# Two more blocks by seven products at two levels, and sums on GpSimd, in an attention and feed-forward kernel

## The chip, the cores and the metric

One core of a Trainium2 chip runs the whole kernel. The metric is device time in microseconds of one execution. All data are float32.

## What is computed

```python
def reference(q, k, v, g_norm, w_in, w_out, s, b):      # q, k, v: (8, 8, 576, 64)
    kv = np.einsum('bhsd,bhse->bhde', k, v)
    out = np.einsum('bhsd,bhde->bhse', q, kv)
    rms = np.sqrt(np.mean(out * out, axis=-1, keepdims=True) + 1e-06)
    x = (out / rms * g_norm).transpose(0, 2, 1, 3).reshape(4608, 512)
    h = x @ w_in                                        # (4608, 512) @ (512, 2048)
    r = np.maximum(h, 0.0)
    return (s * (r * r) + b) @ w_out                    # (4608, 2048) @ (2048, 512)
```

The attention has no softmax: per batch and head a 64x64 matrix kv, and its product with q, normalized row by row. Then comes a feed-forward layer of width 2048 whose activation is an affine function of the squared ReLU.

## The kernel before

**Units.** The 4608 tokens are done in nine units of 512. The code counts them u = 0 to 8; the text calls them units 1 to 9. A unit has a first half (x to the hidden activations, `mm1`) and a second half (hidden to output, `mm2`). Beside them, with steps placed by hand, runs the attention of the next unit (`attention_of_two`, L517, for two pairs of 128 tokens called A and B): turn, product, back, square, row sum, norm, turn_x, scale. The kv product of a batch (`kv_product`, L366) is done where it is due.

**Seven products.** Each matrix product is done by a scheme with seven products of half-size blocks in place of eight. With A the weights and B the activations, cut into 2 x 2 blocks, the products are numbered 1: A11 B11, 2: A12 B21, 3: S4 B22, 4: A22 T4, 5: S1 T1, 6: S2 T2, 7: S3 T3. S1 to S4 are sums of blocks of A, T1 to T4 of B (T1 = B12 - B11, T2 = B22 - T1, T3 = B22 - B12, T4 = B21 - T2). In PSUM one accumulator takes products 1, 6, 5, 3 in that order and is read off after each; a second takes 7 and 4, and product 2 has its own.

**First half of units 3 to 9** (`mm1_deep`, L815 to L1055). The hidden width is cut into four slices s = 0 to 3, which make two pairs, 0 (slices 0, 1) and 1 (slices 2, 3). `x1`, `x6`, `x5` (L849 to L868) do products 1, 6, 5 of one slice, each with four matmul instructions of 256 columns. `small(i, pair, *ms)` (L889) does product i (2, 3, 4 or 7) of both slices of a pair at once, by the scheme a second time: its seven small products m are two matmul instructions of 128 columns each. Before the change, products 2 and 3 are done so for both pairs and 4 and 7 for pair 0; `y7` and `y4` (L859, L877) do 7 and 4 for slices 2 and 3 one slice at a time, four instructions of 256 columns each. The list of those done twice is `DEEP` (L314); their weight sums (two parts each, `sums_of_w_in`, L786) are computed in unit 2, stored to DRAM, and read back in each later unit.

The activations T4 and T3 of a unit are `xs_4` and `xs_7`, computed at the end of the unit before (`x_sums`, L609). `sums_of_x` and `sums_of_xs(i)` (L820, L837) compute the second level's sums of them, four operations each, into tiles `sub`. The hidden blocks are `a11`, `a21`, `a12`, `a22`; `a12` and `a22` (L870, L873) add the parts, `s1` and `s3` (L882, L886) make the sums that the second half needs. Two operations for each slice (square and affine, `done`, L963) are ScalarE's.

**Banks.** `small` for products 2 and 3 writes its first accumulator to one bank (`sx_ps`, a single buffer) and the second to another (`z_ps`, single); a new m = 1 must wait until m = 3 of the call before has been read, and a new m = 2 or 7 until the `z` use before has been read. For product 4 the accumulators are in two buffers `st_ps`, for 7 in two buffers `y_ps`.

**Order.** Nothing is scheduled: each engine executes its instructions in the order in which the code issues them, and waits for what an instruction needs. `run` (L968) is that order for the first half; `at(n)` are the attention's steps, listed in `sides` (L1765 on). The second half starts with `rest` (L1431), into which the last calls of `small` are threaded (`p3_5`, `p3_34`). It ends with four groups of four output stores (`store`, L1269).

**Queues.** SP's queue reads weights through a ring of 14 slots (`pump`, L1088, in the order of `queue_w2`, L1081; a slot is given back in that order by `used`, L1117). GpSimd's queue issues the reads of q (`loads`, L1689; 16 or 32 transfers for one call), the output stores, in unit 2 the stores of weight sums of the second half (`parts_of_w`, L1155), and two memsets a unit (`start_5`, L1395).

Of the kernel before, what the change touches and what calls it, by code (L numbers as in the profile page):

```python
# [17 lines left out]
def kernel(  # L18
# [240 lines left out]
    def add(o, a, b):  # L259
        nc.vector.tensor_tensor(out=o, in0=a, in1=b, op=ALU.add)  # L260

    def sub(o, a, b):
        nc.vector.tensor_tensor(out=o, in0=a, in1=b, op=ALU.subtract)  # L263
# [50 lines left out]
    DEEP = ((2, 0), (7, 0), (3, 0), (4, 0), (2, 1), (3, 1))  # L314
# [321 lines left out]
    ga, g_pair = {}, {}  # L636
# [27 lines left out]
    def g_tile(name, s):  # L664
        if s % 2 == 0:
            g_pair[name, s // 2] = gp.tile([P, 2, 2, TB], FP32, name=name, tag=name)
        ga[name, s] = g_pair[name, s // 2][:, s % 2]
        return ga[name, s]
# [146 lines left out]
    def mm1_deep(u):  # L815
# [4 lines left out]
        def sums_of_x():  # L820
# [8 lines left out]
            sub(t1, b12, b11)  # L829
            sub(t2, b22, t1)  # L830
            sub(t3, b22, b12)
            sub(t4, b21, t2)
# [4 lines left out]
        def sums_of_xs(i):  # L837
# [4 lines left out]
            sub(t1, b12, b11)  # L842
            sub(t2, b22, t1)
            sub(t3, b22, b12)
            sub(t4, b21, t2)
# [13 lines left out]
        def y7(s):  # L859
            st["y", s] = bank_of("y", "y")  # L860
            mm1_product(7, u, s, st["y", s], True)

        def seventh(s):
            return ga["a22", s] if s < 2 else st["y", s]
# [5 lines left out]
        def a12(s):  # L870
            add(g_tile("a12", s), seventh(s), st["r2", s])

        def a22(s):  # L873
            t = ga["a22", s] if s < 2 else g_tile("a22", s)
            add_relu(t, seventh(s), ga["a21", s])

        def y4(s):  # L877
            mm1_product(4, u, s, st["y", s], False)
            t = g_tile("a12", s)
            add_relu(t, st["y", s], st["r2", s])  # L880

        def s1(s):  # L882
            g_tile("s1", s)
            g_s1(s)

        def s3(s):  # L886
            sub(ga["a21", s], ga["a11", s], ga["a21", s])

        def small(i, pair, *ms):  # L889
            name = {2: "a11", 3: "a21", 4: "a12", 7: "a22"}[i]  # L890
            g = (i, pair)
            apart = g == (4, 0)
            fresh = i == 7
            if fresh and ms[0] == 1:
                for s in (2 * pair, 2 * pair + 1):
                    g_tile(name, s)
# [4 lines left out]
            def w_of(m):  # L901
                s0, s1 = 2 * pair, 2 * pair + 1
                raw = {1: (s0, 0), 2: (s0, 1), 4: (s1, 1)}
                if m in raw:
                    s, k = raw[m]
                    return w_in_deep(i, s)[:, k]
                n, k = {6: (6, 0), 7: (6, 1), 5: (5, 0), 3: (5, 1)}[m]
                return ring[u, g, n][:, k]

            def bank_for(m):  # L910
                if fresh:
                    ps = bank_of(("s", i, m), "y").rearrange("p b (m c) -> p (b m) c", c=P)
                    return ps[:, :2]
# [9 lines left out]
            def keep(n, j, h):  # L923
                tag = f"q{n}t" if apart or fresh else {1: "r14", 2: "r2_2", 4: "q4"}[n]
                st[g, n] = late["tmp"].tile([P, 2, P], FP32, name="r", tag=tag)
                if fresh:
                    nc.scalar.copy(st[g, n], st[g, "x"])  # L927
                else:
                    add(st[g, n], st[g, "x"], to(j, h))

            def last(j, h, ps, r):
                (add if fresh else add_relu)(to(j, h), ps, r)

            for m in ms:
# [4 lines left out]
                w, x = w_of(m), a[i, m]  # L939
# [8 lines left out]
                elif m == 2:  # L948
                    last(0, 0, ps, st[g, 1])
                elif m == 6:  # L950
                    keep(2, 1, 0)
                elif m == 5:
                    keep(4, 1, 1)
                    last(1, 1, st[g, "y"], st[g, 4])
                elif m == 3:
                    if fresh:
# [953 lines left out]
```

## Time and profile before

| | us |
|---|---|
| median of 3 runs (898.35 to 899.75) | 898.79 |
| the profiled execution | 898.25 |
| its span in the profile | 896.5 |
| TensorE busy | 886.0 |
| VectorE, ScalarE, GpSimd busy | 697.4, 353.6, 262.2 |
| start of `x1(0)` of units 3 to 9 in the span | 236.4, 329.2, 424.3, 519.6, 614.7, 710.0, 802.6 |

The page gives each engine's busy time, its share in 40 slices of the span, the chain that ended last, and groups of like instructions with count, busy time, mean duration and the idle time before them with what ended it. The timeline gives start, duration, engine, line and operation, with the idle time in front and its releaser in brackets; a run of like instructions is one row. PE is TensorE, DVE is VectorE, ACT is ScalarE, POOL is GpSimd, and SP is the engine that only issues transfers. The time is about 1.8 us longer than the span.

### The profile page before, as it was taken

The numbers are of one execution on the slowest core, as the hardware profiler recorded it, in microseconds if no ns is written. First come the engines' busy times: TensorE is split into PE (matmuls) and PEld (weight loads), VectorE is DVE, ScalarE is ACT, GpSimd is POOL, SyncE is SP. The second block draws the span as 40 slices with busy tenths as digits, with TensorE's granted clock in tenths as the row PEclk, the third lists the DMA queues.
The fourth block names the chain that finished last, engine by engine and source line by source line (L and its number), as shares of the span: only waits on it lengthen the run. The fifth ranks groups of instructions, "written<-read, shape, count | busy, mean of one in ns | idle before, by whom it ended". The sixth has DMA issues, their size and how long they took to land.

```text
span 896.5 us, 19936 instructions
## 1 busy us (share of the span) xinstructions
PE 886.0 (99%) x7706; PEld 819.3 (91%) x7706; DVE 697.4 (78%) x1374; ACT 353.6 (39%) x612; POOL 262.2 (29%) x493
## 2 busy tenths in 40 slices
PE   7999999999999999999999999999999999999998
PEld 4888888888899999999899999999999999999998
DVE  2898777885697978798778868887879797975696
ACT  2887023522266005630455026601660066105610
POOL 2028057014662024701481027403520300021000
PEclk9999999999999999999999999999999999999999
DMA  9897739449963986389646974597639822993286
GB/s 263 310 336 234 197 93 289 162 129 346 305 191 102 311 299 190 87 267 329 215 100 207 310 253 110 153 318 244 186 106 305 294 75 60 301 312 93 60 283 188
DMA packets 124109, 192.96 MB, mean 215 GB/s; under 512 B 25712, under 2 KB 43504, under 8 KB 124016
## 3 DMA queue, kind: packets, MB, share of 16 engines
q1 hardware_dynamic: 104048, 165.84, 57.9%
q0 software_dynamic: 16512, 23.63, 9.3%
q10 hardware_dynamic: 3456, 2.23, 1.0%
q8 instruction: 61, 1.00, 0.5%
q14 instruction: 32, 0.26, 0.1%
HBM read 164.37 MB, written 27.26 MB: 214 GB/s over the span
## 4 chain that ended last, share of the span: by engine, by line
PE 95%; DVE 3%; DMA 1%; ACT 0%; issue 0%; SPq 0%; DVEq 0%
PE x_ps L92 47%; PE y_ps L92 25%; PE z_ps L92 11%; PE sx_ps L92 6%; PE st_ps L92 2%; PE y_ps L553 2%; PE kv_ps L385 2%; DMA kv_sb<-in_v_dram 1%; DVE xT L597 0%; DVE xn L586 0%; DVE xs L263 0%; DVE xn L474 0%; SPq L107 0%; PE z_ps L385 0%; DVE ss L464 0%
## 5 line engine op out<-in xcount | busy, mean ns | idle before, releaser
L1693 POOL DMA_DIRECT2D q_sb<-in_q_dram x296 | 167.1, 572 | 83.1 <-ACT r L927 43.2
L1273 POOL DMA_DIRECT2D out_dram<-o x120 | 59.4, 502 | 358.7 <-issue 210.5
L92 PE MATMUL x_ps<-w_sb,sub 128*128 128x128 f32 x1176 | 148.5, 275 | 0.0
L92 PEld LDWEIGHTS x_ps<-w_sb,sub 128*128 128x128 f32 x1176 | 139.8, 192 | 0.0
L652 ACT ACTIVATE a<-a,b_col,s_col 128x512 f32<-128x512 f32 x144 | 117.1, 814 | 26.9 <-DVE a L655 18.6
L852 ACT COPY a<-x_ps 128x512 f32<-128x512 f32 x28 | 16.3, 581 | 243.1 <-PE x_ps L92 243.1
L92 PE MATMUL x_ps<-xs,ws_raw 128*128 128x256 f32 x384 | 91.4, 381 | 0.1
L92 PE MATMUL x_ps<-xT,wa 128*128 128x256 f32 x360 | 84.1, 382 | 0.1
L92 PE MATMUL y_ps<-xs,wb 128*128 128x256 f32 (+1 forms) x360 | 80.0, 365 | 0.0
L92 PEld LDWEIGHTS x_ps<-xs,ws_raw 128*128 128x128 f32 x384 | 69.5, 190 | 8.5 <-ACT r L726 0.5
L92 PEld LDWEIGHTS x_ps<-xT,wa 128*128 128x128 f32 x360 | 66.6, 190 | 10.7 <-issue 1.7
L965 ACT ACTIVATE a<-a 128x512 f32<-128x512 f32 x112 | 69.5, 621 | 5.5 <-DVE a L267 5.5
L92 PEld LDWEIGHTS y_ps<-xs,wb 128*128 128x128 f32 x360 | 62.9, 190 | 9.1 <-issue 2.3
L92 PE MATMUL x_ps<-w_sb,a 128*128 128x128 f32 (+1 forms) x432 | 64.9, 298 | 0.0
L92 PE MATMUL y_ps<-w_sb,a 128*128 128x128 f32 (+1 forms) x416 | 62.4, 295 | 0.0
L92 PEld LDWEIGHTS x_ps<-w_sb,a 128*128 128x128 f32 x432 | 58.4, 192 | 2.9 <-issue 0.4
L92 PEld LDWEIGHTS y_ps<-w_sb,a 128*128 128x128 f32 x416 | 56.0, 192 | 2.1
L260 DVE TENSOR_TENSOR r<-sx_ps,a 128x256 f32<-128x256 f32 x84 | 35.2, 419 | 23.4 <-PE sx_ps L92 23.3
L260 DVE TENSOR_TENSOR r<-x_ps,o 128x256 f32<-128x256 f32 (+1 forms) x84 | 29.6, 353 | 28.5 <-PE x_ps L92 27.8
L92 PE MATMUL y_ps<-w_sb,sub 128*128 128x128 f32 x392 | 49.5, 275 | 0.0
L92 PE MATMUL z_ps<-w_sb,a 128*128 128x128 f32 (+1 forms) x352 | 46.9, 280 | 0.0
L263 DVE TENSOR_TENSOR a<-a,a 128x512 f32<-128x512 f32 x72 | 46.7, 683 | 0.1
(232 smaller groups left out, 1645.9 us busy)
## 6 DMA issues: line engine op xcount, KB each, us to landing
w_sb<-w SPq DMA_DIRECT2D x427, 256.0 KB, 4.9
w_sb<-w SPq DMA_DIRECT2D x14, 512.0 KB, 8.0
w<-sub POOLq DMA_DIRECT2D x28, 256.0 KB, 5.0
out_dram<-o POOLq DMA_DIRECT2D x112, 64.0 KB, 4.2
w_sb<-in_k_dram SPq DMA_DIRECT2D x24, 288.0 KB, 4.6
w_sb<-in_v_dram SPq DMA_DIRECT2D x24, 288.0 KB, 4.7
w_raw<-in_moe_w_in_dram SPq DMA_DIRECT2D x6, 1024.0 KB, 9.0
q_sb<-in_q_dram POOLq DMA_DIRECT2D x160, 32.0 KB, 3.8
```

The costliest lines, as they stand in the source:

```text
L92: nc.tensor.matmul(o, lhsT=lhsT, rhs=rhs, start=start, stop=stop, skip_group_check=True)
L260: nc.vector.tensor_tensor(out=o, in0=a, in1=b, op=ALU.add)
L263: nc.vector.tensor_tensor(out=o, in0=a, in1=b, op=ALU.subtract)
L385: nc.tensor.matmul(ps[r][(r ^ l) * HB : (r ^ l) * HB + HB, i, :], lhsT=kv[l][0][rows, j, :], rhs=kv[l][1][rows, j, :], start=(j == 0), sto ...
L553: nc.tensor.matmul(ps[l][32 * p : 32 * p + 32, r, lo:hi], lhsT=bd_kv[b % 2][rows, p, at : at + 32], rhs=st["qT"][rows, p, lo:hi], start=Tr ...
L652: nc.scalar.activation(t, t, AF.Identity, scale=s_col, bias=b_col)
L852: nc.scalar.copy(g_tile("a11", s), st["x", s])
L965: nc.scalar.square(ga[name, s], ga[name, s])
L1273: queues[s % 2].dma_start(out=view[b, jj, :, cols], in_=st[name, j][s * w : s * w + w, cols])
L1693: load()
```

## The change

In units 3 to 9, products 7 (S3 T3) of both pairs are done by the scheme twice and in lockstep (`seven`, with a full bank for both pairs), and product 4 (A22 T4) of pair 1 also by `small`; `y7` and `y4` go. `DEEP` grows by (7, 1) and (4, 1), whose sums unit 2 computes in its second half. The twelve sums of x, and s1 and s3 of slices 0 and 1, are GpSimd's. The order in `run` is new; the last two small products of (4, 1) move into `rest` (`p4_34`); the reads of q that were at step 15 are at 18; the kv product of unit 4 is later (`kv3`). Kept parts of product 4 and 7 share buffers, and one of the second half's moves to the buffer `rb`.

```diff
@@ -311,7 +311,7 @@
 
     w2_dram = [dram.tile([P, 2, FC // 2, P], FP32, name=f"w2_{i}") for i in range(8)]
     w3_dram = [dram.tile([P, 4, FC // 4, P], FP32, name=f"w3_{i}") for i in range(8)]
-    DEEP = ((2, 0), (7, 0), (3, 0), (4, 0), (2, 1), (3, 1))
+    DEEP = ((7, 0), (7, 1), (2, 0), (3, 0), (4, 0), (2, 1), (4, 1), (3, 1))
...
@@ -662,7 +662,11 @@
         affine(t)
 
     def g_tile(name, s):
-        if s % 2 == 0:
+        if name == "a22":
+            if s == 0:
+                g_all[0] = gp.tile([P, 2, 2, 2, TB], FP32, name=name, tag=name, bufs=1)
+            g_pair[name, s // 2] = g_all[0][:, s // 2]
+        elif s % 2 == 0:
             g_pair[name, s // 2] = gp.tile([P, 2, 2, TB], FP32, name=name, tag=name)
         ga[name, s] = g_pair[name, s // 2][:, s % 2]
         return ga[name, s]
@@ -826,10 +830,10 @@
                 late["sub"].tile([P, FC // 4, P], FP32, name="sub", tag="sub", bufs=6) for _ in range(2)
             ]
             (t1, t2), (t3, t4) = ((x[:, :2], x[:, 2:]) for x in t)
-            sub(t1, b12, b11)
-            sub(t2, b22, t1)
-            sub(t3, b22, b12)
-            sub(t4, b21, t2)
+            sub(t1, b12, b11, nc.gpsimd)
+            sub(t2, b22, t1, nc.gpsimd)
+            sub(t3, b22, b12, nc.gpsimd)
+            sub(t4, b21, t2, nc.gpsimd)
...
@@ -856,61 +860,79 @@
             st["r2", s] = rp.tile([P, 2, TB], FP32, name="r2", tag="ra" if s % 2 else "rb")
             nc.scalar.copy(st["r2", s], st["x", s])
-        def y7(s):
-            st["y", s] = bank_of("y", "y")
-            mm1_product(7, u, s, st["y", s], True)
-
-        def seventh(s):
-            return ga["a22", s] if s < 2 else st["y", s]
+        def seven(*ms):
+
+            if ms[0] == 1:
+                for t in range(NS):
+                    g_tile("a22", t)
+
+            def to(j, h):
+                return g_all[0][:, :, j, :, h * P : h * P + P]
+
+            def keep(n):
+                st[7, n] = late["tmp"].tile([P, 2, 2, P], FP32, name="r", tag="q2t" if n == 2 else "q14t")
+                nc.scalar.copy(st[7, n], st[7, "x"])
+
+            for m in ms:
+                first = m in (1, 2, 7)
+                if first:
+                    ps = bank_of(("s", 7, m), "y").rearrange("p b (m c) -> p (b m) c", c=P)
+                    st[7, "x" if m == 1 else "y"] = ps.rearrange("p (i b) c -> p i b c", b=2)
+                ps = st[7, "x" if m in (1, 6, 5, 3) else "y"]
+                for pair in range(2):
+                    w = w_deep(7, pair, m)
+                    for b in range(2):
+                        matmul(ps[:, pair, b], w[:, b], a[7, m], first and pair + b == 0, True)
+                    if m in (7, 3):
+                        used((u, (7, pair), 6 if m == 7 else 5))
+                if m == 1:
+                    keep(1)
+                elif m == 2:
+                    add(to(0, 0), ps, st[7, 1])
+                elif m == 6:
+                    keep(2)
+                elif m == 5:
+                    keep(4)
+                    add(to(1, 1), st[7, "y"], st[7, 4])
+                elif m == 3:
+                    nc.scalar.copy(to(0, 1), ps)
+                elif m == 4:
+                    add(to(1, 0), ps, st[7, 2])
 
         def x5(s):
             mm1_product(5, u, s, st["x", s], False)
             nc.scalar.copy(g_tile("a21", s), st["x", s])
 
         def a12(s):
-            add(g_tile("a12", s), seventh(s), st["r2", s])
+            add(g_tile("a12", s), ga["a22", s], st["r2", s])
 
         def a22(s):
-            t = ga["a22", s] if s < 2 else g_tile("a22", s)
-            add_relu(t, seventh(s), ga["a21", s])
-
-        def y4(s):
-            mm1_product(4, u, s, st["y", s], False)
-            t = g_tile("a12", s)
-            add_relu(t, st["y", s], st["r2", s])
-
-        def s1(s):
-            g_tile("s1", s)
-            g_s1(s)
-
-        def s3(s):
-            sub(ga["a21", s], ga["a11", s], ga["a21", s])
+            add_relu(ga["a22", s], ga["a22", s], ga["a21", s])
+
+        def s1(s, engine=nc.vector):
+            add(g_tile("s1", s), ga["a21", s], ga["a22", s], engine)
+
+        def s3(s, engine=nc.vector):
+            sub(ga["a21", s], ga["a11", s], ga["a21", s], engine)
+
+        def w_deep(i, pair, m):
+            s0, s1 = 2 * pair, 2 * pair + 1
+            raw = {1: (s0, 0), 2: (s0, 1), 4: (s1, 1)}
+            if m in raw:
+                s, k = raw[m]
+                return w_in_deep(i, s)[:, k]
+            n, k = {6: (6, 0), 7: (6, 1), 5: (5, 0), 3: (5, 1)}[m]
+            return ring[u, (i, pair), n][:, k]
         def small(i, pair, *ms):
-            name = {2: "a11", 3: "a21", 4: "a12", 7: "a22"}[i]
+            name = {2: "a11", 3: "a21", 4: "a12"}[i]
             g = (i, pair)
-            apart = g == (4, 0)
-            fresh = i == 7
-            if fresh and ms[0] == 1:
-                for s in (2 * pair, 2 * pair + 1):
-                    g_tile(name, s)
+            apart = i == 4
...
-            def w_of(m):
-                s0, s1 = 2 * pair, 2 * pair + 1
-                raw = {1: (s0, 0), 2: (s0, 1), 4: (s1, 1)}
-                if m in raw:
-                    s, k = raw[m]
-                    return w_in_deep(i, s)[:, k]
-                n, k = {6: (6, 0), 7: (6, 1), 5: (5, 0), 3: (5, 1)}[m]
-                return ring[u, g, n][:, k]
-
             def bank_for(m):
-                if fresh:
-                    ps = bank_of(("s", i, m), "y").rearrange("p b (m c) -> p (b m) c", c=P)
-                    return ps[:, :2]
...
             def keep(n, j, h):
-                tag = f"q{n}t" if apart or fresh else {1: "r14", 2: "r2_2", 4: "q4"}[n]
-                st[g, n] = late["tmp"].tile([P, 2, P], FP32, name="r", tag=tag)
-                if fresh:
-                    nc.scalar.copy(st[g, n], st[g, "x"])
+                if apart:
+                    t = late["tmp"].tile([P, 2, 2, P], FP32, name="r", tag="q2t" if n == 2 else "q14t")[:, 0]
                 else:
-                    add(st[g, n], st[g, "x"], to(j, h))
-
-            def last(j, h, ps, r):
-                (add if fresh else add_relu)(to(j, h), ps, r)
+                    t = late["tmp"].tile(
+                        [P, 2, P], FP32, name="r", tag={1: "r14", 2: "r2_2", 4: "q4"}[n]
+                    )
+                st[g, n] = t
+                add(t, st[g, "x"], to(j, h))
...
-                w, x = w_of(m), a[i, m]
+                w, x = w_deep(i, pair, m), a[i, m]
...
@@ -968,25 +986,30 @@
         def run(at, early):
             x1(0)
             at(2)
+            sums_of_xs(7)
+            sums_of_x()
+            sums_of_xs(4)
+            seven(1)
             x1(1)
-            sums_of_x()
+            seven(2)
             small(2, 0, 1, 2)
             x6(0)
+            seven(6)
             at(4)
             at(5)
-            sums_of_xs(7)
-            small(7, 0, 1, 2)
+            seven(7)
             small(2, 0, 6, 7)
             at("kv")
             x6(1)
-            small(7, 0, 6, 7)
+            seven(5)
             at(6)
             small(2, 0, 5)
             x5(0)
             at(7)
-            small(7, 0, 5)
+            seven(3)
             small(2, 0, 3, 4)
-            small(7, 0, 3, 4)
+            seven(4)
+            at("kv3")
             a12(0)
             a22(0)
             small(3, 0, 1, 2)
@@ -1006,51 +1029,53 @@
             at(12)
             small(3, 0, 3, 4)
             done("a22", 1)
-            sums_of_xs(4)
             x6(2)
             at(13)
             small(4, 0, 1, 2)
-            y7(2)
+            x6(3)
             done("a21", 0, 1)
             at(14)
             small(4, 0, 6, 7)
             small(2, 1, 1, 2)
-            x6(3)
-            s1(0)
+            a12(2)
+            s1(0, nc.gpsimd)
+            x5(2)
             at(15)
             small(4, 0, 5)
             small(2, 1, 6, 7)
-            s1(1)
-            x5(2)
+            s1(1, nc.gpsimd)
+            a12(3)
+            x5(3)
             small(4, 0, 3, 4)
             small(2, 1, 5)
             a22(2)
-            y7(3)
-            s3(0)
+            s3(0, nc.gpsimd)
             done("a12", 0, 1)
+            small(4, 1, 1, 2)
             small(2, 1, 3, 4)
+            a22(3)
             at(16)
-            x5(3)
             done("a22", 2)
-            s3(1)
+            s3(1, nc.gpsimd)
             done("a11", 2, 3)
-            a22(3)
+            small(3, 1, 1, 2)
+            small(4, 1, 6, 7)
             early()
             at(18)
-            y4(2)
             done("a22", 3)
-            small(3, 1, 1, 2)
-            done("a12", 2)
-            y4(3)
             small(3, 1, 6, 7)
-            done("a12", 3)
+            small(4, 1, 5)
 
         def rest_of_3():
             small(3, 1, 3, 4)
             done("a21", 2, 3)
 
+        def rest_of_4():
+            small(4, 1, 3, 4)
+            done("a12", 2, 3)
+
         last = dict(
-            p3_5=lambda: small(3, 1, 5), p3_34=rest_of_3,
+            p3_5=lambda: small(3, 1, 5), p3_34=rest_of_3, p4_34=rest_of_4,
             s1=lambda: (s1(2), s1(3)), s3=lambda: (s3(2), s3(3)),
         )
         return run, last
@@ -1078,7 +1103,11 @@
         if u == 1:
             queue_w2 += [(u, i, n) for i in (1, 2, 6, 7, 5, 3, 4) for n in range(2)]
         else:
-            queue_w2 += [(u, key, m) for key in DEEP for m in (6, 5)]
+            first = [((7, p), m) for m in (6, 5) for p in range(2)]
+            first[2:2] = [((2, 0), 6)]
+            first += [((2, 0), 5)]
+            queue_w2 += [(u, *k) for k in first]
+            queue_w2 += [(u, key, m) for key in DEEP[3:] for m in (6, 5)]
             queue_w2 += [(u, i, m) for i, m in ORDER]
@@ -1221,7 +1250,10 @@
 
             def keep(name, j, q):
                 if name == "r2":
-                    r[name] = late["tmp"].tile([P, n, P], FP32, name="r", tag=f"r2_{n}")
+                    if n == 1:
+                        r[name] = rp.tile([P, 2, TB], FP32, name="r", tag="rb")[:, :1, :P]
+                    else:
+                        r[name] = late["tmp"].tile([P, n, P], FP32, name="r", tag="r2_2")
                 else:
@@ -1431,6 +1463,7 @@
         def rest():
             do_1(1)
             start_5()
+            step["p4_34"]()
             step["p3_5"]()
             sums_1((5, 6))
-            return first, second
+            return first, {7: of[12:13], 8: of[13:14], 9: of[14:15], 11: of[15:]}
-            "kv": kv if u not in (2, 5) else [],
+            "kv": kv if u in (4, 6) else [],
+            "kv3": kv if u == 3 else [],
-            15: q[1],
+            18: q[1],
```

The two functions `sums_of_x` and `sums_of_xs` take `nc.gpsimd` for all four of their operations; `add` and `sub` have a new argument for the engine.

## Prediction

> **What bounds the kernel now.** First the page: which engine is full, and whether the chain that ends last is that engine.
>
> ```profile
> PE 886.0 (99%) x7706; PEld 819.3 (91%) x7706; DVE 697.4 (78%) x1374; ACT 353.6 (39%) x612; POOL 262.2 (29%) x493
> PE   7999999999999999999999999999999999999998
> ...
> PE 95%; DVE 3%; DMA 1%; ACT 0%; issue 0%; SPq 0%; DVEq 0%
> ```
>
> TensorE is busy for 886.0 of 896.5 us, in all but the first and last slices at nine tenths or more, and it is 95% of the chain. From 40 to 800 us the windows show it idle for under 0.1 us. So the time is TensorE's work; it falls by what is taken off TensorE, and grows by every wait that the change puts in front of TensorE, which has none in units 3 to 9 today.
>
> Second, the groups by shape and the timeline of TensorE, for the price of a multiplication.
>
> ```profile
> L92 PE MATMUL y_ps<-xs,wb 128*128 128x256 f32 x304 | 72.0, 380 | 0.0
> L92 PE MATMUL y_ps<-xs,wb 128*128 128x128 f32 x56 | 8.0, 286 | 0.0
> ```
> ```profile
> 375.70 0.61 PE L92 MATMUL sx_ps<-xT,ws_raw 128*128 128x128 f32 x4
> 376.15 0.61 PE L92 MATMUL z_ps<-xT,ws_raw 128*128 128x128 f32 x4
> 376.60 1.89 PE L92 MATMUL y_ps<-xs,wb 128*128 128x256 f32 x8
> 378.32 0.61 PE L92 MATMUL sx_ps<-sub,w_sb 128*128 128x128 f32 x4
> ```
>
> The means (380, 286 ns) overlap; the price is the distance between starts. Four records of 128 columns take 0.446 us, eight of 256 columns 1.73 us: 0.1116 and 0.216 us a record. One matmul instruction leaves two records, so the four instructions of one `y4` cost 1.73 us and two of `small` 0.446.
>
> **TensorE's part.** Each of units 3 to 9 loses `y7` and `y4` of slices 2 and 3: 4 x 1.73 = 6.9 us. It gains the seven small products of S3 T3 and of A22 T4 for the second pair: 2 x 7 x 2 instructions x 2 records x 0.1116 = 6.25 us. That is 0.65 us a unit and **4.6 us** in seven units, certain if nothing waits. Everything else on TensorE is only reordered.
>
> **VectorE and ScalarE.** Per unit VectorE loses twelve sums of x (4 x 0.42 + 8 x 0.28) and four of 0.68 (half of S1 and S3), 6.6 us; it gains seven operations of 0.42 for the small products of A22 T4, and 3 x 0.26 since the adds of S3 T3 grow from 256 to 512 columns: 3.7 us. The two `a12` adds replace two add-relus. It is lighter by 3 us of 95, worth nothing by itself, because no TensorE wait on it exists to be shortened. ScalarE's copies grow by 0.8 us of 36.6 in 95: free. In unit 2 VectorE does eight more sums of 0.42 (3.4 us) where its timeline shows idle stretches of 6.0 and 2.0 us, and SP four more stores: free.
>
> **Transfers.** Four more reads of 256 KB in each of units 3 to 9, 1 MB in 95 us, with the DMA engines at 0.70 of their time over a unit. The ring of 14 slots issues them units of several us ahead, against a median of 4.9 us to landing. Free, with one place to watch: in unit 4 the kv product moves to `kv3`, and the first slots it frees (after half its 2.27 us) must be refilled for `small(3, 0, 6, 7)`, 4.9 us after it starts. A 4.9 us landing would be 1.1 us late, once; I take 0 and keep 1.1 for the range.
>
> **First new wait: S3 T3's sixth small product waits for GpSimd.** `seven(6)` needs T2 of `xs_7`, two GpSimd operations, and GpSimd's queue holds in front of them the last output stores of the unit before. Today these sums are on VectorE. The order of starts in a unit, from T0 (its `x1(0)`): x1(0) 1.73, seven(1) 0.89, x1(1) 1.73, seven(2) 0.89, small(2,0,1,2) 0.89, x6(0) 1.73: `seven(6)` is due at T0 + 7.86. GpSimd's timeline around the start of unit 3, whose T0 is 236.42:
>
> ```profile
> 240.15 1.96 POOL L1273 DMA_DIRECT2D out_dram<-o  x4 [1.88 <-DVE sub L263]
> 242.10 2.17 POOL L1170 DMA_DIRECT2D w<-sub  x4
> 246.13 0.51 POOL L1273 DMA_DIRECT2D out_dram<-o  x1 [1.86 <-DMA out_dram<-o]
> 247.34 1.48 POOL L1273 DMA_DIRECT2D out_dram<-o  x3 [0.70 <-DMA out_dram<-o]
> ```
> and of unit 4, T0 329.18:
> ```profile
> 329.20 3.91 POOL L1273 DMA_DIRECT2D out_dram<-o  x8 [3.97 <-DVE o L260]
> 335.56 1.96 POOL L1273 DMA_DIRECT2D out_dram<-o  x4 [2.44 <-DMA out_dram<-o]
> ```
>
> The last four stores wait for earlier ones to land, in every unit, and the queue is free only at 248.82, 337.52, 432.27, 526.35, 622.53, 716.77, 809.90; `seven(6)` is due at 244.28, 337.04, 432.19, 529.7 (unit 6 has its kv product before it), 622.57, 717.81, 810.41.
>
> The trace has no two-input operation on GpSimd. Nearest rows: a memset of 128x128 at 0.204 us and of 128x512 at 0.520, and an affine select of 128x128, one input, at 0.288. Bounds for 128x128: 0.20 and 0.52. I take 0.35, nearest the affine select, with a second input to read. Two of them and the 0.1 us between a result and TensorE's start (0.06 to 0.15 in the first 30 us) make 0.8. Lateness: 5.3, 1.3, 0.9, 0, 0.8, 0, 0.3 = **8.6 us** (7.1 at 0.20, 10.4 at 0.52). The later sums have cover: T3 is due 2 us later, and T2 of x 2.9 us later.
>
> The Trainium skill, "GPSIMD Engine Reference", section on performance versus the Vector engine, puts a two-input operation at about 2.6 cycles of 1.2 GHz per element and calls GpSimd the wrong choice for ordinary elementwise work; for 128 elements that is an estimated 0.28 us and a dispatch, with which this term would be 8 to 9 us. No run here shows it yet. The same skill's "SBUF — State Buffer" (who interferes with whom) says that a VectorE operation with two SBUF inputs blocks and is blocked by a GpSimd operation that reads SBUF; the trace of before, where GpSimd computes nothing, cannot show it.
>
> **Second new wait: one PSUM bank, no cover.** The first pair's and second pair's small products of A12 B21 and S4 B22 share the single `sx` and `z` banks. Before, `small(2,1,3,4)` is followed by `x5(3)` and `y4(2)`, 3.45 us, and then `small(3,1,1,2)`. After, `small(3,1,1,2)` comes straight behind: its first product overwrites `sx`, which VectorE must first have read (the add-relu of `small(2,1,3)`). VectorE's spacing, from before:
>
> ```profile
> 368.94 0.42 DVE L267 CUSTOM_DVE_ANT_1 a<-st_ps,a 128x256 f32<-128x256 f32 x1 [1.26 <-PE st_ps L92]
> 369.38 0.42 DVE L267 CUSTOM_DVE_ANT_0 a<-st_ps,r 128x256 f32<-128x256 f32 x1
> 369.83 0.42 DVE L260 TENSOR_TENSOR r<-sx_ps,a 128x256 f32<-128x256 f32 x1
> 370.29 0.42 DVE L267 CUSTOM_DVE_ANT_0 a<-z_ps,r 128x256 f32<-128x256 f32 x1
> 370.63 0.68 DVE L267 CUSTOM_DVE_ANT_0 a<-y_ps,a 128x512 f32<-128x512 f32 x1
> ```
>
> 0.34 us to an independent operation, 0.46 to a dependent one, 0.60 behind one of 512 columns; a result is picked up 0.2 us after TensorE's last start. Set t = 0 at the end of small(4,0,3). TensorE: small(4,0,4) to 0.45, (2,1,5) 0.89, (4,1,1) 1.34, (4,1,2) 1.79, (2,1,3) 2.23, (2,1,4) 2.68: `small(3,1,1)` is due at 2.68. VectorE's queue: (4,0,3) at 0.2, (4,0,4) 0.65, (2,1,5) 1.09 and 1.55, a22(2) 1.89, (4,1,1) 2.49, (4,1,2) 2.95, (2,1,3) 3.29, done 3.71. With 0.1 to start: 1.1 us late, in all seven units, **7.7 us**. With VectorE fully caught up it would be 0.2 + 0.42 + 0.06 - 0.45 = 0.25 each, 1.8 us: the lower bound.
>
> **Third: small(3,0,1).** It needs `sx` read by small(2,0,3). VectorE now does the row sum (issue 1.14) behind the add of seven(5), which waits for a ScalarE copy. From the start of seven(6), by the same spacings: copy done 9.54, add 9.58, row sum 10.18, small(2,0,5) 11.32 and 11.78, reciprocal and norm 12.12 and 12.40, small(2,0,3) 13.54, done 13.95. TensorE is due at 13.65: 0.35 to 0.4 late with the start, in the six units with attention beside them, **2.1 us** (0 to 4).
>
> **Moved, and covered.** S1 and S3 of the first pair go to GpSimd (about 1.1 us each by the same reckoning): S1 is read by sums 15 us later. The q reads behind them now issue at about T0 + 41 and take 17.3 us (32 issues), so the two memsets behind the reads move from T0 + 50 to T0 + 58.6; the add that needs them stands at 389.26, T0 + 60. Cover 1.5 us. If GpSimd is slower than that, VectorE's dense stretch after it slips, and TensorE with it.
>
> **Sum.** 898.25 (the profiled execution's own time, 0.5 under the median of 898.79, less than my terms are worth) - 4.6 + 8.6 + 7.7 + 2.1 = **912.0 us**, slower by 1.5%. With all low bounds 898.25 - 4.6 + 7.1 + 1.8 = 902.5; with all high ones (10.4, 1.6 each for the bank, 4, 1.1) about 920.
>
> **Rivals.**
> - *The handoffs are covered* (0.12). The place is the two handoffs to TensorE, GpSimd to `seven(6)` and VectorE to `small(3,1,1)`; only their bare latency shows, 0.25 x 7. 898.25 - 4.6 + 1.8 = 895.5, faster. It decides once GpSimd is free by T0 + 7.0 in every unit and all waits together stay under 2.8 us. For it: VectorE loses 3 us a unit, TensorE's order has slack everywhere today. Against it: unit 3's 12.4 us.
> - *Only the stores of unit 2 count* (0.13). VectorE is ahead of my reckoning, and in later units the stores land sooner: 5.3 + 1.8 - 4.6 = +2.5, 900.7, from 897 to 902.5.
> - *GpSimd is the bound of the second half too* (0.07): operations held up by VectorE's, memsets late by 2 us a unit: 912 + 14 = 926.
> - The forecast has 0.68. That the change doesn't do what it says is excluded: the order of TensorE's instructions shows the 56 records a unit.
>
> About 0.2% is what a measurement of this kernel can tell from no change: 1.8 us, 897.0 to 900.6. Faster 0.12, same 0.08 (the lower part of the second rival), slower 0.80. The range 897 to 920 leaves out the first rival and the last, 0.19.
>
> **What would show it.** Right: TensorE's busy time down by some 4 us without the waits, an idle stretch before `y_ps<-sub,w_sb` near 244 us released by GpSimd, and one before the `sx_ps<-xT,ws_raw` of small(3,1,1) in each unit released by VectorE. Wrong: a TensorE timeline without holes there, GpSimd's first `sub` of unit 3 before 244, or holes before DMA-loaded weights.

## The result and the profile after

The kernel after takes **931.83 us** (median of 4 runs, 925.48 to 937.18) where the kernel before takes 899.13 beside it: 1.036 times as long, 95% interval 1.029 to 1.043. It is slower, as forecast, but by 33 us and not by 13, and outside the range of 897 to 920. The profiled execution took 933.1 us with a span of 931.2.

The page of after: busy times, TensorE's slices, the granted clock, the chain.

```profile
PE 896.9 (96%) x7874; PEld 829.5 (89%) x7874; DVE 697.7 (75%) x1319; ACT 362.4 (39%) x612; POOL 345.9 (37%) x605
...
PE   7999999999799999999999999999999999999998
...
PEclk9999999999899999999999999999999999999999
...
PE 29%; DVE 3%; DMA 1%; POOL 1%; issue 0%; ACT 0%; DVEq 0%; POOLq 0%; ACTq 0%
```

TensorE still is the bound by share, yet its busy time rose by 10.9 us, though its work fell by 4.6, and its idle time by 23.8. One slice, near 250 us, holds a hole and a lower clock. The chain is followed over only a third of the span; it is no guide here, and the waits are read instead. TensorE's waits in after (us in all, times, longest):

```profile
PE y_ps L92 <- POOL sub L263: 8.1, 5, 5.7
PE sx_ps L92 <- DVE a L267: 7.1, 7, 1.0
PE x_ps L92 <- DVE r L260: 6.4, 3, 2.3
```

The first two rows are the first and second new wait of the forecast. The third was not in its sum: it is the add that needs the memsets, late in units 4, 5 and 6. Those three, with 0.3 for an `sx_ps` wait for GpSimd, are 21.9 of the 23.8 us. Most of the rest is 0.67 us before `small(3,0,6)` of unit 4 and 0.90 us at the kv product just before unit 3, which waits for v and did not wait before:

```profile
234.59 1.26 PE L385 MATMUL kv_ps<-w_sb 64*64 64x64 f32 x68 [0.90 <-DMA w_sb<-in_v_dram]
```

So `x1(0)` of unit 3 starts at 237.61 us where it started at 236.42.

The first wait in unit 3, in the timelines of GpSimd and TensorE:

```profile
248.79 1.50 POOL L1305 DMA_DIRECT2D out_dram<-o  x3 [0.59 <-DMA out_dram<-o]
250.31 0.47 POOL L263 TENSOR_TENSOR sub<-xs 128x128 f32<-128x128 f32 x1
250.85 0.46 POOL L263 TENSOR_TENSOR sub<-xs,sub 128x128 f32<-128x128 f32 x1
```
```profile
251.36 2.07 PE L92 MATMUL y_ps<-sub,w_sb 128*128 128x128 f32 x8 [5.72 <-POOL sub L263]
```

The last three stores, two sums of 0.46 us, and `seven(6)`. But its eight records now take 2.07 us, not 1.05. The windows around it say why (columns: stretch, length, TensorE busy, granted clock, DMA share, GB/s):

```profile
248.00:249.00 1.00, 0.00 (x0) 0.96 1.07 426
249.00:250.00 1.00, 0.00 (x0) 0.50 1.02 383
...
254.00:255.00 1.00, 1.00 (x50) 0.50 0.00 0
255.00:256.00 1.00, 1.00 (x29) 0.63 0.00 0
```

Some 3 us into the wait the clock went to a half, and stayed there for 4.4 us after the wait was over. So a wait is paid for twice. The same happened at all three memset waits. Unit 4, GpSimd, VectorE, TensorE:

```profile
379.41 2.96 POOL L260 TENSOR_TENSOR s<-a,a 128x512 f32<-128x512 f32 x2 [8.34 <-ACT a L652]
...
385.22 9.60 POOL L1726 DMA_DIRECT2D q_sb<-in_q_dram  x18
...
404.93 0.58 POOL L1430 MEMSET o<- 128x256 f32 x2
```
```profile
405.29 0.42 DVE L260 TENSOR_TENSOR r<-x_ps,o 128x256 f32<-128x256 f32 x1 [2.98 <-POOL o L1430]
```
```profile
405.77 3.66 PE L92 MATMUL x_ps<-w_sb,sub 128*128 128x128 f32 x16 [2.25 <-DVE r L260]
```

S1 and S3 of slices 0 and 1 hold GpSimd to 385.22, the q reads to 404.93, then come the memsets that VectorE and TensorE wait for; the sixteen records behind take 3.66 us where 1.95 is usual.

**Where 34.7 us of span went.** Waits that the profile shows: 8.4 + 7.1 + 6.4 + 1.9 of others = 23.8. TensorE's work: -4.6. Records at half clock: 4.4 us in unit 3 and about 3.4 behind each memset wait, half of it lost: some 7. The rest is **late starts** that no row shows as idle, since a row's end is modelled. They are found from the distance between starts, less 0.1116 us for each record of 128 columns and 0.216 for each of 256. In unit 7 of after they come to 3.7 us, of which the profile calls 2.1 idle; in unit 5 of before to 0.6, none of it idle. That is about 1 us a unit more. The lengths of units 3 to 9, from `x1(0)` to `x1(0)`, say the same: they grew by 33.6 us in all, and with 4.6 less work, 23 of waits and 7 of slow clock some 8 us are left. The four terms make 34.2.

### The profile page after: what moved, and what is told of

Read it like the earlier page. It is cut to its first block, busy times and chain, and to the rows that moved or that the text cites. A ratio compares the mean times of both kernels' runs of the same rounds, so it can differ in the third digit from the quotient of the medians.

```text
span 931.2 us, 20471 instructions
## 1 busy us (share of the span) xinstructions
PE 896.9 (96%) x7874; PEld 829.5 (89%) x7874; DVE 697.7 (75%) x1319; ACT 362.4 (39%) x612; POOL 345.9 (37%) x605
## 5 line engine op out<-in xcount | busy, mean ns | idle before, releaser
L92 PE MATMUL x_ps<-w_sb,sub 128*128 128x128 f32 x1176 | 152.7, 280 | 6.5 <-DVE r L260 6.4
L92 PEld LDWEIGHTS x_ps<-w_sb,sub 128*128 128x128 f32 x1176 | 143.2, 196 | 7.3 <-DVE r L260 7.0
L260 DVE TENSOR_TENSOR a<-y_ps,r 128x512 f32<-128x512 f32 x31 | 21.3, 688 | 55.2 <-PE y_ps L92 27.8
L92 PEld LDWEIGHTS y_ps<-w_sb,sub 128*128 128x128 f32 x392 | 48.0, 197 | 0.0
L260 POOL TENSOR_TENSOR s<-a,a 128x512 f32<-128x512 f32 x14 | 20.1, 1433 | 74.6 <-ACT a L652 74.0
```

Source lines behind the costliest of these rows:

```text
L92: nc.tensor.matmul(o, lhsT=lhsT, rhs=rhs, start=start, stop=stop, skip_group_check=True)
L260: engine.tensor_tensor(out=o, in0=a, in1=b, op=ALU.add)
```

## The experiments

**One wait at a time.** The first four kernels ran on one chip. Memsets:

```diff
-                nc.gpsimd.memset(slot(j, 3), 0.0)
+                nc.vector.memset(slot(j, 3), 0.0)
```

> Only the two memsets of slot 3 go from GpSimd to VectorE, so they no longer stand behind the q reads. Theory (a wait of its own size, and behind a wait of about 2 us some microseconds of TensorE at half its clock): the three x_ps waits of 1.8 to 2.3 us in units 4, 5 and 6 go (6.4 us idle), and so do the stretches of granted clock 0.5 behind them, about 1.6 us each: 11 to 12 us less, span about 919 to 920, the clock of 1.0 in units 4 to 6. Rival 'waits only' (the clock falls for another reason): 6 to 7 us less, about 924.5, and the clock still falls in units 4 to 6. Rival 'a late input' (the memset was not what was late): no change.

920.81 us (920.64 to 921.07): 11.0 less. The three waits are gone and the clock is 1.0 in units 4 to 6. More than the 6.4 us of idle time came back, so the clock's part is real. The spread of the runs fell from 11.7 us to 0.4.

```diff
-            sub(t1, b12, b11, nc.gpsimd)      # and the other three, in sums_of_x and sums_of_xs
+            sub(t1, b12, b11)
```

> The twelve sums of x of each unit go back to VectorE; S1 and S3 of slices 0 and 1 stay on GpSimd. Theory: the waits of y_ps and sx_ps for a subtraction of GpSimd go (8.4 us idle, 5.7 of it in unit 3), and the 6 us at half clock in unit 3 (about 3 us lost): 11 to 12 us less, span about 919 to 920. Rival 'waits only': 8.4 less, 922.8, with the clock still low near 250 us. Rival 'VectorE is full': its 12 added subtractions of 0.28 to 0.42 us per unit (some 3.9 us) come back as waits for VectorE: under 6 us less.

923.7 us: 8.1 less. The small waits of the later units went, but unit 3 kept 5.2 us, now released by VectorE. None of the three theories had that. Not all of the 8.1 belongs to the sums: behind two of the three memset waits, 1.85 and 2.02 us long, the clock stayed at 1.0 in the profiled execution.

```diff
-            small(3, 1, 1, 2)
             small(4, 1, 6, 7)
+            small(3, 1, 1, 2)
```

> One swap in the order: products 6 and 7 of A22 of the second pair run ahead of products 1 and 2 of A21 of the second pair, which puts 8 instructions (0.9 to 1.8 us) between the last reader of the sx bank and the product that waits for it. Theory: the seven waits of 1.0 us go (7.1 us idle, and 0.1 to 0.26 us more of each in stretched rows): 7 to 9 us less, about 922.5 to 924; the clock does not change, since it did not fall behind waits of 1.0 us. Rival 'VectorE is late by more': the wait is met again at the next bank, under 3 us less.

930.57 us: 1.3 less, which is small against the 11.7 us over which the runs of after spread. My theory failed; the rival had under 3 us. The idle row fell from 7.1 to 2.2 us, but by the distances between starts the place cost 1.26 us a unit where it had cost 1.27: 0.28 before `small(4,1,6)`, 0.22 before `small(3,1,1)`, 0.48 before `small(3,1,6)`, and three of about 0.1. The wait was only cut into pieces too small for an idle row.

> The three edits together; S1 and S3 of slices 0 and 1 stay on GpSimd. Theory: the parts add, 29.5 to 32.5 us less: span 898.5 to 901.5, and clock 1.0 from end to end. By the other road, the kernel before less its shorter TensorE work, 4.6, and 2.1 of small waits for the sums: about 896, so 896 to 901. Rival 'waits only': 22 us less, 909. Rival 'the two elementwise engines get in each other's way or the added DMAs do': over 905, with VectorE's same-shaped rows longer than in the kernel before.

916.66 us, 15.2 less, not 30. Two causes stand in its trace. In unit 3, VectorE ahead of the first sum of `xs_4`, and what waits for VectorE:

```profile
251.96 0.29 DVE L263 TENSOR_TENSOR sub<-xs 128x128 f32<-128x128 f32 x1 [9.30 <-DMA w<-sub]
```
```profile
253.64 2.08 PE L92 MATMUL y_ps<-sub,w_sb 128*128 128x128 f32 x8 [5.02 <-DVE a L260]
```

The sums of `xs_7`, for which `seven(6)` had waited in after, are done on VectorE at 241.19. Behind them, the sum of `xs_4` needs a `sub` tile that one of unit 2's last stores of weight sums has yet to free, and that store is on GpSimd's queue between the output stores: it is issued at 244.44 and lands at 251.93. Until then VectorE does nothing of what stands behind that sum. So here too the queue of stores is the cause, and not the engine that adds. The second, in the row of small products at the end of the first half, GpSimd above and VectorE below:

```profile
476.21 2.95 POOL L260 TENSOR_TENSOR s<-a,a 128x512 f32<-128x512 f32 x2 [5.31 <-ACT a L652]
```
```profile
476.40 1.62 DVE L260 TENSOR_TENSOR a<-a,r 128x512 f32<-128x512 f32 x1
...
479.25 1.68 DVE L260 TENSOR_TENSOR a<-a,r 128x512 f32<-128x512 f32 x1
```

Two adds of VectorE with both inputs in SBUF take 1.6 to 1.7 us while GpSimd adds; 0.68 is usual. It happens twice in every unit of after as well, 14 adds and 13.5 us of VectorE in all; adds with one input in PSUM keep their 0.42.

**Is it the hold-ups, or VectorE's load?**

```diff
-            s1(0, nc.gpsimd)                  # and s1(1), s3(0), s3(1)
+            s1(0)
```

> The three edits, and S1 and S3 of slices 0 and 1 on VectorE as well, so GpSimd computes nothing. With the three edits alone the time was 916.7, not 896 to 901, and in its trace the two adds of A12 for slices 2 and 3, which read two SBUF tiles, took 1.62 to 1.75 us in each unit, 0.68 elsewhere, while GpSimd worked on S1. Theory 'the two engines hold each other up': this gives VectorE back 1.96 us a unit and costs it 4 x 0.68 = 2.7, of which half falls after the small products; the 128x512 adds are all at 0.68 to 0.69, and the time falls by 2 to 6 us, to 911 to 915. Rival 'VectorE simply has too much work there': the 2.7 us weigh more, 917 to 922. Unit 3's wait of 5 us stays in both.

925.56 us: 8.9 slower than with S1 and S3 on GpSimd, though all adds are at 0.68. The hold-up theory is refuted as the main cost, and the rival was right and too mild: 2.7 us a unit more of VectorE, of which the adds gave back 2.0, cost 1.3 us a unit of time. In this order off-loading them was a gain.

**Other orders.** The edits of the next two, beside the above:

```diff
-            sums_of_xs(4)                     # behind sums_of_x()
+            sums_of_xs(4)                     # ahead of x1(2)
-            seven(3)
             small(2, 0, 3, 4)
+            seven(3)
-            x5(3)                             # behind a12(3)
+            x5(3)                             # behind small(2, 1, 3, 4); a22(3) behind small(3, 1, 1, 2)
```

> Nothing on GpSimd, and three moves in the order instead of the swap: the sums of xs_4 wait until x1(2) (unit 3: VectorE stood 9.3 us before them, for a sum tile that a store on GpSimd's queue still had to free); small(2,0,3,4) runs ahead of seven(3); x5(3) runs behind small(2,1,3,4), so that its 1.73 us of TensorE stand ahead of small(3,1,1), and a22(3) behind small(3,1,1,2). Theory (all that is left are handoffs in time): unit 3's 5.0 us and some 3 us of low clock go, 0.3 a unit of small(3,0,1), and about 1 us a unit in the row of small products: 8 + 2 + 7 below the three edits, 897 to 903. Rival 'the row of small products is limited by VectorE, at 0.34 to 0.46 us an operation against 0.446 of TensorE': moves inside it only move the wait, 905 to 910.

> The same order with S1 and S3 of slices 0 and 1 on GpSimd. Theory 'the two engines hold each other up': two adds of VectorE at 1.6 to 1.7 us again in each unit, 14 us of VectorE in all, at the row of small products: 1 to 6 us slower than the same order with nothing on GpSimd. Rival 'off-loading helps': 1 to 4 us faster, since VectorE loses 2.7 us a unit.

915.67 and 917.23 us, the first above the ranges of its theory and of its rival. With the sums of `xs_4` moved, unit 3's wait and its low clock are gone, in these and in all later kernels: that cause is shown. The late starts are not gone: 3.3 us in unit 5 of the first of the two, at new places (0.90 before `small(2,0,3)`, 0.77 before `small(4,1,1)`, 0.43). In this order S1 and S3 on GpSimd cost 1.6 us on balance, where in the order before they had gained 8.9: what they are worth depends on the order.

**The clock by itself.** Sums of `xs_7` in units 4 to 9 on GpSimd behind repeats of the first one:

```diff
+            for _ in range((0, 0, 0, 0, 2, 6, 2, 8, 16)[u] if i == 7 else 0):
+                sub(t1, b12, b11, engine)
```

> The same order with nothing on GpSimd but the four sums of xs_7 in units 4 to 9, behind 0, 2, 6, 2, 8 and 16 repeats of their first subtraction (0.46 us each), so that TensorE meets waits before seven(6) of about 0.7, 1.2, 2 to 3, 1.9, 3.6 and 7.7 us. Theory 'the granted clock falls behind a long wait': it stays 1.0 behind the first two, falls to about 0.5 for 3 to 4 us behind those from 1.8 us on, and for 6 to 7 us behind the longest ones, each time beginning 2 to 3 us after the wait began. Rival 'the clock falls for a load that has nothing to do with the waits': no fall there, or falls elsewhere.

TensorE's rows behind four of the six waits, and the windows at the second of these:

```profile
440.48 1.16 PE L92 MATMUL y_ps<-sub,w_sb 128*128 128x128 f32 x8 [1.11 <-POOL sub L263]
...
638.59 1.60 PE L92 MATMUL y_ps<-sub,w_sb 128*128 128x128 f32 x8 [1.94 <-POOL sub L263]
...
743.32 2.08 PE L92 MATMUL y_ps<-sub,w_sb 128*128 128x128 f32 x8 [5.56 <-POOL sub L263]
...
849.09 3.79 PE L92 MATMUL y_ps<-sub,w_sb 128*128 128x128 f32 x16 [8.50 <-POOL sub L263]
```
```profile
638.00:639.00 1.00, 0.41 (x3) 1.00 0.00 0
639.00:640.00 1.00, 1.00 (x7) 0.57 0.00 0
```

Behind waits of 0.50, 1.07 and 1.11 us the clock stayed at 1.0. Behind 1.94 it was 0.5 for 3.4 us (639.1 to 642.6), which began only after TensorE had started again; behind 5.56 for 6.8 us, behind 8.50 for 10.2. After the two long waits the slow time outlasted the wait by 5 us. The one execution took 941.08 us, 25.5 more than the profiled execution of the same order without the repeats (915.55). The six waits come to 18.7 us, and half of the slow time in which TensorE worked, 3.4 and twice 5.0 us, to 6.8: together 25.5. So the slow clock is paid for at half of its length.

**Less on VectorE in the row.** The next two keep the swap and the later sums of `xs_4`, sums and memsets on VectorE, and S1 and S3 on GpSimd; `x5(1)` goes ahead of `small(3,0,1,2)`. The first also moves two adds:

```diff
-            add(g_tile("a12", s), ga["a22", s], st["r2", s])
+            add(g_tile("a12", s), ga["a22", s], st["r2", s], nc.vector if s < 2 else nc.gpsimd)
```

> Result so far: S1 and S3 of slices 0 and 1 on VectorE cost 9 us against the three edits alone (925.6 against 916.7), though they free its adds from GpSimd: the row of small products at the end of a unit's first half is VectorE's to pace. So here VectorE is relieved in it: sums of x on VectorE (those of xs_4 at x1(2)), S1 and S3 of slices 0 and 1 and the two adds of A12 of slices 2 and 3 on GpSimd, memsets on VectorE, x5(1) ahead of small(3,0,1,2), and small(4,1,6,7) ahead of small(3,1,1,2). Theory 'VectorE paces the row': per unit its two adds of 1.65 us leave the row, so the waits there (about 1.2 us a unit with the three edits) shrink to 0.1 to 0.3 us, the 0.4 of small(3,0,1) goes, and unit 3's 5 us with its low clock go: 916.7 - 6 to 8 - 2.5 - 8 = 898 to 901. Rival 'the row is bound by the latency of one handoff after the other, whatever VectorE's load': 904 to 908.

> The same, but with the two adds of A12 of slices 2 and 3 on VectorE, where GpSimd's S1 holds them at 1.6 to 1.7 us. Theory 'VectorE paces the row': 5 to 8 us slower than with them on GpSimd, 904 to 908. Rival 'handoffs': within 2 us of it.

908.59 and 908.11 us: equal within 0.5 us, as the rivals had it, and just above the 904 to 908 of the first one's rival. The two adds stand ahead of the stretch in which VectorE is full; with them on GpSimd it only idles for 1.85 us there. No wait over 0.5 us is left in units 3 to 9 of the first (the second has one of 1.06, for weights in unit 4), and yet the late starts are 2.43 us a unit (0.58 before): 7 x 1.85 - 4.6 + 898.25 = 906.6, near the 908.7 of its profiled execution; another 1.5 us lie before unit 3. So nearly the whole loss in units 3 to 9 is late starts. Those in the row come where VectorE is busy for 5.29 of 5.64 us (stretch, length, VectorE busy, granted clock, DMA share, GB/s):

```profile
568.36:574.00 5.64, 5.29 (x13) 1.00 0.68 167
```

**One part alone.** S3 T3 in lockstep, A22 T4 of the second pair as a plain product again, with nothing on GpSimd:

```diff
+        def y4(s):
+            ps = bank_of(("y", s), "y")
+            mm1_product(4, u, s, ps, True)
+            add_relu(ga["a12", s], ps, ga["a12", s])
...
+            y4(2)                             # behind early()
...
+            y4(3)                             # behind small(3, 1, 1, 2)
```

> One part alone: S3 T3 of both pairs in lockstep, but A22 T4 of the second pair as a plain product (two of 1.73 us a unit instead of seven small pairs of 0.446), in the kernel before's order behind step 14, and nothing on GpSimd. TensorE's work is 898.25 - 7 x (0.65 - 0.34) = 896.1. Theory 'the row of small products is what costs': the 1.3 us a unit of handoffs there go, those of the first half stay (0.27 + 0.11 + 0.09 a unit, 3 us): 899 to 901, the same as before within 0.3%. Rival 'lockstep is what costs (eight banks' worth of handoffs in the first half)': 904 or more.

917.98 us. Part of it was my order, which put dependent products side by side; x6(3), x5(3) and the norm moved for a second trial:

> S3 T3 in lockstep alone, once more: in the first trial of it the order put small(4,0,6,7) straight behind small(4,0,1,2) and small(2,1,3) straight behind small(2,1,5), and it was there that TensorE started late, by 0.93 + 0.21 and 0.68 us a unit. Here x6(3) and x5(3) stand between them, and the norm behind small(3,0,1,2). Theory 'order': 918.0 - 7 x 1.8 to 2.1 = 903 to 905.5; with TensorE's work at 896 and 0.9 us a unit of small handoffs left. Rival 'lockstep itself costs': 912 or more.

917.34 us. The late starts moved (0.87 before `small(3,0,5)`, 0.47 before a product of the second half) and the time did not, as the rivals of both trials had it. Whether lockstep alone can be made free stays open; in two orders it was not.

**The whole, spaced out.** In the row, x5(3), a22(2), `small(4,0,3,4)`, `small(2,1,5)`, `small(4,1,1,2)`, `small(2,1,3,4)`, `small(4,1,6,7)`, `small(3,1,1,2)`, a22(3), `small(4,1,5)`, `small(3,1,6,7)`, the early sums; then once more with two moves mended:

> Both parts, with the row spaced out: in the row each bank's next product now has 0.89 to 1.34 us of others between it and the last (small(4,1,5) between small(3,1,1,2) and small(3,1,6,7)), a22(2) goes where VectorE stood idle for 1.85 us, a22(3) and the early sums go behind; the norm goes behind small(2,0,3,4). The two adds of A12 and S1, S3 of slices 0 and 1 on GpSimd, sums of x and memsets on VectorE. Theory 'a handoff through VectorE takes 0.7 us and is hidden by two products of 0.446 us if VectorE is free': of 2.4 us of extra starts a unit some 1.0 to 1.5 go, 7 to 10 us less than the 908.6 of the version without this order: 898 to 902. Rival 'VectorE is full there in any order': 904 to 908.

> The version with the row spaced out left no extra start of TensorE in the row itself, but 0.84 us a unit before product 6 of small(3,0) (the norm of VectorE ran behind seven(4) and ahead of the read of small(3,0,1)) and 0.79 before the first product that takes the early sums (they ran last). Here the norm follows small(3,0,1,2), whose bank has x5(1) for cover, the early sums go ahead of small(3,1,6,7), and a22(3) goes behind it. Theory 'a handoff of 0.7 us, hidden or not by what stands between': both go, 7 x (0.6 + 0.7) = 9 less than 910.3: 900 to 903. Rival 'VectorE is full in the row, the wait goes to another bank': 906 to 910.

910.26 and 914.15 us, above the ranges of both theories and of both rivals. The row itself has no late start any more, but 0.79 us a unit came back behind it, at a product that needs a sum of VectorE, and stayed when the early sums were moved. The norm, moved on, made 0.87 us at the next bank.

**Work or handoffs?** The last two leave out two adds of VectorE in each unit, and with them a part of the result:

```diff
-            a22(2)
-            a22(3)
```

> The version with the row relieved (908.6), with the two adds of A22 of slices 2 and 3 left out (so part of the result is not computed): 2 x 0.68 us of VectorE less in the row of each unit, TensorE's instructions and their order the same. Its late starts in the row were 0.28, 0.22 and 0.48 us a unit, and some 0.3 in smaller ones. Theory 'VectorE's throughput in the row': the first two go and the third falls to 0.25 (a bare handoff behind one product of 0.446), 0.7 a unit: 903 to 904.5. Rival 'bare handoffs': within 1 us of 908.6.

> The version with the row spaced out (910.3), with the same two adds left out (part of the result is not computed). Its row had no late start, but 0.79 us a unit just behind it, before the first product that takes a sum of VectorE, and 0.84 in the first half, which the adds do not touch. Theory 'VectorE's throughput': the 0.79 goes, 5 to 5.5 us: 904.5 to 906. Rival 'that sum is late for another reason': within 1 us of 910.3.

904.78 and 907.51 us, 3.8 and 2.8 less than with them; the first is 0.3 above the range of its theory. The same rows of TensorE, with the adds and without (start, duration):

```profile
570.39 0.61 PE L92 MATMUL z_ps<-sub,wa 128*128 128x128 f32 x4
571.12 1.27 PE L92 MATMUL st_ps<-sub,w_sb 128*128 128x128 f32 x8
572.23 0.61 PE L92 MATMUL sx_ps<-xT,ws_raw 128*128 128x128 f32 x4
```
```profile
568.88 0.61 PE L92 MATMUL z_ps<-sub,wa 128*128 128x128 f32 x4
569.33 1.06 PE L92 MATMUL st_ps<-sub,w_sb 128*128 128x128 f32 x8
570.22 0.61 PE L92 MATMUL sx_ps<-xT,ws_raw 128*128 128x128 f32 x4
```

From start to start 0.73 and 1.11 us with them, 0.45 and 0.89 without: the 0.28 and 0.22 are gone, and the 0.48 behind them is 0.30, as the theory of throughput said. In the second, the 0.79 fell to 0.33, not to nothing, and the time stays 1.5 us above the theory's 906. So more than half of the late time in the row is VectorE's amount of work there; the remaining 0.3 is about what the spacings give for a bare handoff behind a single product of 0.446 us, which no run shows by itself. No version that computes everything came below the kernel before; the best were at 908.

## Why the prediction was right and wrong

- **Direction, and TensorE's part.** Right in direction, and for the reason given: waits that outweigh the work saved. The 4.6 us cannot be read off directly, but the 906.6 worked out with them is within 2.1 of that kernel's run.
- **First new wait.** Right in size: 8.1 against 8.6 (and 0.3 at another of GpSimd's sums in unit 9), unit 3 at 5.7 against 5.3, the others 0.73, 0.28, 0, 0.97, 0, 0.41. GpSimd's 128x128 sum took 0.46, inside the bounds, where 0.35 was taken. The reason was right: the output stores stand ahead of the sums on GpSimd's queue. Its price was wrong, since the clock was left out. And the same stores had a second way into unit 3, through the tile of the `xs_4` sums, which held VectorE for as long once the sums were there.
- **Second.** 7.1 idle and 0.17 more a unit in late starts, 8.3, against 7.7. The size was right, the place too; that cover alone would cure it was not (1.3 us from the swap).
- **Third.** 0.25 us, and 0.10 at the record behind it, against 0.35, in five units and not in six.
- **"Moved, and covered" failed.** The step said that the memsets shift to T0 + 58.6, with 1.5 us of cover. They ended at T0 + 66 in unit 4. S1 began only at T0 + 39.9, behind ScalarE; the four sums took 1.46 us each, not 1.1; the reads took 19.7 us, not 17.3. The 1.46 is longer than the 1.27 that one such add took alone on GpSimd. This is the last rival's mechanism, which had 0.07: 6.4 us of waits and 11.0 of time, in three of the seven units.
- **The missing term.** No step asked what a wait does to TensorE afterwards. By the runs, half clock behind four waits, some 7 us.
- **Transfers, put at nothing.** The wait for weights in unit 4, kept for the range at 1.1 us, came: 0.67 us in after, where the profile names VectorE, and 0.40 to 1.21 in all of the experiments but one, released by the read of weights. The work that unit 2 gained was called free; unit 3 starts 1.2 us later, 0.90 of it the wait for v. Which of the added transfers makes v late was not tried.
- **The late starts.** The sum took VectorE as 3 us a unit lighter and looked at three handoffs one by one. VectorE's busy time did not fall (697.4 us before, 697.7 after), 13.5 us of it being the held-up adds, and in the row it is full: the plain products that the change takes away (four of 1.73 us a unit) were work of TensorE with no read of 128x256 after every 0.446 us. Some 8 us in after, of which the forecast had the 2.1 of its third handoff.

With these, 912.0 - 2.1 + 6.4 + 7 + 8 + 1.6 = 932.9, against 933.1 measured in the profiled execution.

The prediction cited the Trainium skill, "SBUF — State Buffer" (who interferes with whom), for a mutual block. The trace of after shows it, 1.55 to 1.69 us against 0.68 for the adds with two SBUF inputs. In the time it weighed far less than the 13.5 us that the rows add up to: with the same sums on VectorE the kernel was 1.6 us faster in one order and 8.9 slower in another, and with the held-up adds moved away it was equal.

## What to carry to other kernels

A long product that is replaced by short ones takes away cover as well as work: count how much of the engine that reads the banks falls into the same stretch, before and after, and not only the handoffs. An engine that issues transfers in order is late by all of them, so what is put ahead of a queue of reads is late for everything behind it. A wait of TensorE of 2 us or more should be priced with the half clock behind it.

## What the hardware showed that was not expected

The clock of TensorE fell to a half behind waits of 1.78 us and more, and not by their length alone: of ten waits between 1.78 and 2.41 us after the first 30 us of all runs, six had it (1.78, 1.80, 1.94, 2.25, 2.32, 2.41) and four had not (1.83, 1.85, 2.02, 2.26); all of 5 us and more had it; none up to 1.54. It came back after about 3.4, 6.8 or 10.2 us. The Trainium skill, "TensorE: Matmul & The Clock Gate" (Part 1), tells of a free-running activity window of about 3.4 us and warns of idle gaps above that; the steps of 3.4 us agree, while here gaps of 1.8 us were enough at times. That the fall depends on where a wait lies in such a window would also explain why the runs of after spread over 11.7 us, and those of the first experiment, where the waits near 2 us are gone, over 0.4; this is argued, not shown.

An add of GpSimd took 0.46 us for 128 columns, 0.73 for 256 and 1.27 for 512 when alone, against 0.28, 0.42 and 0.68 on VectorE.
